# One row of W_down, loaded by transfers of 95 and 33 partitions, in a decode layer on one core

## The chip, the core and the metric

The kernel runs on one core of one Trainium2 chip. A core has a matrix engine (TensorE, PE in the profile; its weight loads are PEld), a vector engine (VectorE, DVE), a scalar engine (ScalarE, ACT), GpSimd (POOL) and a sync engine (SyncE, SP), which here only issues transfers. Sixteen DMA engines move data between HBM and SBUF. The metric is the device time of one execution, in microseconds.

## The reference

One decode step of a transformer layer, for 4 sequences with one new token each: attention over a cached window, then a gated MLP.

```python
# x: [4, 1, 576]; k_cache, v_cache: [4, 16, 16384, 128]; all bfloat16
q = layernorm(x) @ wq                  # 32 heads of 128
k, v = the last 4096 positions of the caches, each of the 16 heads used by 2 query heads
p = softmax(q k^T / sqrt(128))
h = x + (p v) @ wo
g = layernorm(h)
gate = g @ W_gate; up = g @ W_up       # [576, 4608] each
out = h + ((gate * (gate > 0)) * up) @ W_down      # W_down: [4608, 576]
```

The window of the two caches is 134 MB, wq and wo are 4.7 MB each, and W_gate, W_up and W_down 5.3 MB each. All of it is read once.

## The kernel before

All weights and the caches go through one large SBUF buffer, `pool`, of four slots. SP issues the loads one after the other, in the order of the list `transfers`, each when the part of the buffer that it overwrites is free: wq (two transfers), then 32 transfers of 4096 KB that alternate between a K and a V block of four heads, then wo, then W_gate and W_up (two transfers each), and at the end W_down in six pieces. Each entry of the list has a name, the key of a semaphore, what must have been done before it is issued, and a function that issues it. `prog_sync` walks through the list; the store of the result stands behind it in the same queue and waits for OUT0 and OUT1.

For each of the 16 K blocks, DVE transposes the block (L403), PE multiplies it with the queries (L466 and L468 are the helper that records every PE operation), DVE takes the row maximum, ACT the exponential, DVE transposes the probabilities, and PE multiplies them with the V block. After the last block PE multiplies with wo (the end of this is ATTN), DVE and ACT compute the second layer norm, PE multiplies with W_gate and W_up, ACT and DVE form the gated product `hh`, and DVE transposes it into `hhT`.

W_down is seen as 128 partitions of 36 rows of 576 values (1152 bytes): row j of partition p is row 36 p + j of the matrix. `WD` cuts the 36 rows into six pieces of 14, 9, 6, 4, 2 and 1 rows, each loaded by one transfer of all 128 partitions with a semaphore of its own (`wd0` to `wd5`). All six are issued by SP once ATTN is done, since they overwrite the region from which wo was read. PE's last loop goes through the pieces in that order: it waits for the landing of a piece and then makes two matmuls for each of its rows, which add up in PSUM. After the last row, ACT and DVE copy the two halves of the result to SBUF (OUT0, OUT1), and SP stores it.

A transfer's semaphore counts to 16 for each transfer. The method `dma` of the class `Sched` adds 16 to the count of the key at each issue, and a wait for a name waits for the count which that key has after the named transfer. So a wait for the last of three transfers with one key is a wait for 48.

Of the kernel before, what the change touches and what calls it, by code (L numbers as in the profile page):

```python
# [12 lines left out]
D = 576  # L13
# [24 lines left out]
JJ = 36  # L38
# [63 lines left out]
def bass_sequential_preLN__sliding_block_cached__glu_gated_reglu__decode_kernel(  # L102
# [12 lines left out]
    with ExitStack() as es:  # L115
        cnt = [0]

        def sb(name, shape, dt):
            return es.enter_context(nc.sbuf_tensor(name, shape, dt))

        pool = sb("pool", [128, NSLOT * QUAD], BF16)
# [79 lines left out]
        transfers = []  # L201
# [49 lines left out]

        wd_sb = pool[:, 0:FC * D].rearrange("p (j n) -> p j n", j=JJ)
        WD = [(0, 14), (14, 23), (23, 29), (29, 33), (33, 35), (35, 36)]
        for k, (f0, f1) in enumerate(WD):
            transfers.append((("wd", k), f"wd{k}", ["ATTN"],
                              lambda e, f0=f0, f1=f1: e.dma_start(
                                  out=pool[:, f0 * D:f1 * D], in_=B_W_down.rearrange("(p j) n -> p (j n)", j=JJ)[:, f0 * D:f1 * D])))

        def feat(c):
            return slice(c, c + 509, 4) if c < 4 else slice(512, D)  # L260
# [1 line left out]
        def land(name):  # L262
            return ("L",) + (name if isinstance(name, tuple) else (name,))
# [195 lines left out]
        def prog_pe(S):  # L459
# [133 lines left out]

            for k, (f0, f1) in enumerate(WD):
                deps = [land(("wd", k))]
# [44 lines left out]
```

## Time and profile before

| | |
|---|---|
| time, median of 3 runs | 377.71 us (377.62 to 377.88) |
| the profiled execution's own time | 378.56 us |
| its span | 377.2 us |
| PE, PEld busy | 302.2 us (80%), 73.0 us (19%) |
| DVE, ACT, POOL busy | 225.8 us (60%), 53.4 us (14%), 5.2 us (1%) |
| moved by DMA | 159.74 MB, mean 423 GB/s |
| DMA packets | 6506 |
| issue to landing, six pieces of W_down | 15.0, 17.7, 19.3, 20.2, 20.4, 20.3 us |

The span is the time from the first to the last instruction of the profiled execution; the execution's own time has what lies around it too. Busy time is the sum over an engine's instructions, and an engine can be busy without being what the others wait for. The landing of a transfer is the time when its semaphore has its full count. Each DMA packet is recorded with its queue, its start, its duration and its size, but without the number of the DMA engine that carried it.

### The profile page before, as it was taken

The page shows a single profiled execution, that of the slowest core. Times are in us where ns is not written, and L with a number is a line of the kernel's source. Part 1 is how long each engine was busy: PE and PEld are TensorE (multiplying, and loading weights), DVE is VectorE, ACT ScalarE, POOL GpSimd, SP SyncE. Part 2 cuts the span into 40 slices and gives each one's busy share as a digit, 9 for nine tenths or more (in the row PEclk, how much of TensorE's full clock was granted, in tenths as well). Part 3 has the DMA queues.
Part 4 walks back from the last instruction along what each step waited for, and adds up shares of the span by engine and source line. Part 5 has one row for each costly group of instructions (what it writes and reads, how often), then busy time and mean ns, then how long its engine had stood idle before and what let it go on. Part 6 is the DMA issues. An engine that isn't in the chain of part 4 may idle for free.

```text
span 377.2 us, 2603 instructions
## 1 busy us (share of the span) xinstructions
PE 302.2 (80%) x1432; PEld 73.0 (19%) x772; DVE 225.8 (60%) x165; ACT 53.4 (14%) x140; POOL 5.2 (1%) x15
## 2 busy tenths in 40 slices
PE   0509299969996999499969996899879996968667
PEld 0101022212221222022212221122112121212214
DVE  8046677595849493858476846666675768231230
ACT  2202402110220112002200220020202010101020
POOL 5000000000000000000000000000000000000000
PEclk9999789998999899989989997799959998996988
DMA  8999999999999999999999999999999999999996
GB/s 334 445 445 389 445 440 393 445 440 438 422 424 441 438 434 408 441 441 427 413 440 441 431 427 427 440 434 427 420 441 440 417 424 441 422 432 429 443 404 255
DMA packets 6506, 159.74 MB, mean 423 GB/s; under 512 B 728, under 2 KB 864, under 8 KB 1632
## 3 DMA queue, kind: packets, MB, share of 16 engines
q1 hardware_dynamic: 6488, 159.59, 98.8%
q8 instruction: 8, 0.13, 0.1%
q10 hardware_dynamic: 8, 0.00, 0.0%
q14 instruction: 2, 0.02, 0.0%
HBM read 159.58 MB, written 0.00 MB: 423 GB/s over the span
## 4 chain that ended last, share of the span: by engine, by line
DMA 47%; DVE 29%; PE 20%; ACT 3%; SPq 1%; issue 1%; DVEq 0%
DMA pool<-in_A_k_cache_dram 41%; DVE kT L403 20%; PE sc L466 7%; PE sc L468 6%; DMA pool<-in_B_W_down_dram 5%; DVE acc L420 4%; PE val L466 3%; PE val L468 3%; DVE own_sb L417 2%; DVE probT L414 2%; ACT P L338 2%; PE pb L466 1%; DVE o_bf L442 0%; ACT L338 0%; DVE rmx L406 0%
## 5 line engine op out<-in xcount | busy, mean ns | idle before, releaser
L403 DVE STREAM_TRANSPOSE kT<-pool 128x2048 f32<-128x2048 f32 x64 | 142.8, 2278 | 25.3 <-DMA pool<-in_A_k_cache_dram 24.3
L466 PE MATMUL sc<-kT,qz 128*128 128x512 bf16 x256 | 110.5, 432 | 36.6 <-DVE kT L403 36.3
L468 PE MATMUL sc<-kT,qz 128*128 128x512 bf16 x256 | 109.6, 428 | 0.0
L466 PE MATMUL val<-pool,probT 128*64 128x512 bf16 (+2 forms) x328 | 104.2, 374 | 4.4 <-DMA pool<-in_B_W_down_dram 4.4
L468 PE MATMUL val<-pool,probT 128*64 128x512 bf16 x256 | 96.2, 379 | 0.0
L466 PEld LDWEIGHTS sc<-kT,qz 128*128 128x128 bf16 x256 | 26.7, 104 | 146.5 <-issue 71.1
L466 PEld LDWEIGHTS val<-pool,probT 128*64 128x64 bf16 (+1 forms) x328 | 32.1, 107 | 81.3 <-issue 68.5
L406 DVE TENSOR_REDUCE rmx<-sc 128x1 f32<-128x1024 f32 x16 | 19.6, 1225 | 41.0 <-PE sc L468 41.0
L333 ACT ACTIVATE diag<-spot,rmx 128x16 f32<-128x16 f32 x16 | 4.9, 307 | 234.0 <-DVE rmx L406 234.0
L414 DVE STREAM_TRANSPOSE probT<-P 128x1024 bf16<-128x1024 bf16 x16 | 19.9, 1246 | 21.0 <-ACT P L338 21.0
L338 ACT ACTIVATE P<-sc,bias 128x1024 bf16<-128x1024 f32 x16 | 17.8, 1114 | 21.0 <-DVE bias L409 21.0
L327 ACT COPY qz<-qrep 32x128 bf16<-32x128 bf16 x64 | 18.8, 294 | 0.6
L409 DVE TENSOR_REDUCE bias<-pb 128x1 f32<-128x16 f32 x16 | 2.8, 175 | 23.8 <-PE pb L466 23.8
L420 DVE TENSOR_REDUCE acc<-own_sb 128x128 f32<-128x1024 f32 x8 | 15.2, 1897 | 0.3
L417 DVE TENSOR_TENSOR own_sb<-val,mask 128x1024 f32<-128x1024 f32 x8 | 9.6, 1200 | 7.9 <-PE val L468 7.9
L466 PE MATMUL sc<-pool,oX 128*4 128x288 bf16 x32 | 10.0, 338 | 0.4 <-ACT oX L347 0.4
L468 PE MATMUL sc<-pool,oX 128*4 128x288 bf16 x32 | 9.9, 336 | 0.0
L478 PE MATMUL pb<-ident_b,xn_bf 4*128 4x4 bf16 (+1 forms) x5 | 0.4, 180 | 10.0 <-DVE xn_bf L371 10.0
L466 PE MATMUL sc<-qT,sel 32*128 32x128 bf16 x4 | 0.3, 284 | 9.6 <-DVE qT L427 9.6
L445 DVE TENSOR_TENSOR h_row<-sc,x_bf 4x576 f32<-4x576 f32 x1 | 0.7, 745 | 11.6 <-PE sc L468 11.6
L466 PE MATMUL pb<-diag,same 128*128 128x16 f32 x32 | 6.3, 273 | 1.7 <-ACT diag L333 1.7
L466 PEld LDWEIGHTS pb<-diag,same 128*128 128x128 f32 x32 | 4.8, 188 | 11.8 <-ACT diag L333 7.4
(102 smaller groups left out, 85.7 us busy)
## 6 DMA issues: line engine op xcount, KB each, us to landing
pool<-in_A_k_cache_dram SPq DMA_DIRECT2D x16, 4096.0 KB, 26.8
pool<-in_A_v_cache_dram SPq DMA_DIRECT2D x16, 4096.0 KB, 26.4
pool<-in_A_wo_dram SPq DMA_DIRECT2D x1, 4608.0 KB, 18.3
pool<-in_B_W_gate_dram SPq DMA_DIRECT2D x1, 4608.0 KB, 18.6
pool<-in_B_W_up_dram SPq DMA_DIRECT2D x1, 4608.0 KB, 24.7
pool<-in_A_wq_dram SPq DMA_DIRECT2D x1, 4096.0 KB, 12.7
pool<-in_B_W_down_dram SPq DMA_DIRECT2D x1, 2016.0 KB, 15.0
pool<-in_B_W_down_dram SPq DMA_DIRECT2D x1, 1296.0 KB, 17.7
```

The costliest lines, as they stand in the source:

```text
L327: S.op(a, lambda e, src=src, dst=dst: e.copy(out=dst, in_=src), deps=deps, name=("QZ", i) if g == 3 else None, signal=g == 3)
L333: S.op(a, lambda e, i=i: e.activation(out=diag[:, i % 2, :], in_=spot[:, :], func=ACT.Copy, scale=rmx[:, i % 2:i % 2 + 1]), deps=[("RMAX", ...
L338: S.op(a, lambda e, i=i: e.activation(out=Pb[:, (i % 2) * 1024:(i % 2 + 1) * 1024], in_=sc[:, (i % 2) * 1024:(i % 2 + 1) * 1024], func=ACT ...
L403: S.op(v, lambda e: e.transpose(out=dst, in_=src), deps=deps, name=("TR", f))
L406: S.op(v, lambda e: e.tensor_reduce(out=rmx[:, i % 2:i % 2 + 1], in_=sc[:, (i % 2) * 1024:(i % 2 + 1) * 1024], axis=AX.X, op=ALU.max), dep ...
L409: S.op(v, lambda e: e.tensor_reduce(out=bias[:, i % 2:i % 2 + 1], in_=pb[TPB][:, 16 * (i % 2):16 * (i % 2) + 16], axis=AX.X, op=ALU.min), ...
L414: S.op(v, lambda e: e.transpose(out=pT[i % NPT], in_=Pb[:, (i % 2) * 1024:(i % 2 + 1) * 1024]), deps=[("EXP", i)] + ([("PV", i - NPT)] if ...
L417: S.op(v, lambda e: e.tensor_tensor(out=own_sb[:, :].rearrange("p (x d) -> p x d", d=DH), in0=val[:, :].rearrange("p (x d) -> p x d", d=DH ...
L420: S.op(v, lambda e: e.tensor_reduce(out=acc[:, w % 2, :], in_=own_sb[:, :].rearrange("p (x d) -> p d x", d=DH), axis=AX.X, op=ALU.add), de ...
L445: S.op(v, lambda e: e.tensor_tensor(out=h_row[:, :], in0=attn, in1=x_bf[:, :], op=ALU.add), deps=["ATTN", land("x")], name="H")
L466: return e.matmul(o, lhsT=l, rhs=r, start=start, stop=stop, skip_group_check=skip)
L468: return e.add_instruction(mybir.InstMatmult(name=nc.get_next_instruction_name(), start_tensor_calc=start, stop_tensor_calc=stop, bass_ski ...
```

## The change

The third piece of W_down, rows 23 to 28, is loaded as before but for its last row. Row 28 is loaded by two transfers of its own, issued ahead of the rest of the third piece: one for partitions 0 to 94, and one for partitions 95 to 127. All three count on the semaphore `wd2`, so PE's wait for the third piece is now one for a count of 48. The bytes, their places, all other transfers and all instructions of the other engines stay as they were. SP issues 47 loads where it issued 45.

```diff
         wd_sb = pool[:, 0:FC * D].rearrange("p (j n) -> p j n", j=JJ)
         WD = [(0, 14), (14, 23), (23, 29), (29, 33), (33, 35), (35, 36)]
+        wd_src = B_W_down.rearrange("(p j) n -> p (j n)", j=JJ)
+
+        def add_wd(name, key, f0, f1, p0, p1):
+            transfers.append((name, key, ["ATTN"], lambda e: e.dma_start(out=pool[p0:p1, f0 * D:f1 * D], in_=wd_src[p0:p1, f0 * D:f1 * D])))
+
         for k, (f0, f1) in enumerate(WD):
-            transfers.append((("wd", k), f"wd{k}", ["ATTN"],
-                              lambda e, f0=f0, f1=f1: e.dma_start(
-                                  out=pool[:, f0 * D:f1 * D], in_=B_W_down.rearrange("(p j) n -> p (j n)", j=JJ)[:, f0 * D:f1 * D])))
+            if k == 2:
+                add_wd(("wd", 6), "wd2", 28, 29, 0, 95)
+                add_wd(("wd", 7), "wd2", 28, 29, 95, 128)
+            add_wd(("wd", k), f"wd{k}", f0, f1 - (k == 2), 0, 128)
```

## The prediction

> **What bounds the kernel now.** I read the 40 slices first, then the chain of waits, then the timeline and the busy shares of the last ten microseconds, and last the queues and the landings. The slices of the page say that the DMA engines have no gap from the second slice to the last:
>
> ```profile
> DMA  8999999999999999999999999999999999999996
> GB/s 334 445 445 389 445 440 393 445 440 438 422 424 441 438 434 408 441 441 427 413 440 441 431 427 427 440 434 427 420 441 440 417 424 441 422 432 429 443 404 255
> ```
>
> PE and DVE are busy too, but nothing else is full from one end to the other, and only the last slice is half empty. So the time is the bytes at about 425 GB/s, plus what the tail adds. The chain of waits in time, from the issues of W_down on, confirms it:
>
> ```profile
> 353.78 20.18 DMA pool<-in_B_W_down_dram
> 374.00 0.70 PE val L466 x7
> 374.72 0.68 PE val L466 x5
> 375.42 0.42 DVE out_sb L456
> ```
>
> The fourth piece of W_down is in the queue from 353.78 to 373.96; then the fifth and sixth pieces land, PE does their products, DVE and ACT copy the result, and the store ends the span at 377.2. The timeline shows that PE waits for each piece:
>
> ```profile
> 367.48 4.95 PE L466 MATMUL val<-pool,probT 128*4 128x320 bf16 x46 [3.77 <-DMA pool<-in_B_W_down_dram]
> 372.63 0.98 PE L466 MATMUL val<-pool,probT 128*4 128x320 bf16 x12 [0.21 <-DMA pool<-in_B_W_down_dram]
> 374.00 1.38 PE L466 MATMUL val<-pool,probT 128*4 128x320 bf16 x14 [0.39 <-DMA pool<-in_B_W_down_dram]
> 375.42 0.42 DVE L456 CAST out_sb<-val 4x256 bf16<-4x256 f32 x1 [9.02 <-PE val L466]
> ```
>
> The last landing therefore sets the end, with a fixed 2.2 us behind it (375.03 to 377.2). Now the busy shares of that stretch (columns: window, its length, busy time of PE, PEld, DVE, ACT, POOL, then the granted clock, the DMA share and GB/s):
>
> ```profile
> 371.00:373.00 2.00, 1.79 (x26) 1.02 (x23) 0.00 (x0) 0.00 (x0) 0.00 (x0) 1.00 0.98 396
> 373.00:374.00 1.00, 0.61 (x11) 0.25 (x6) 0.00 (x0) 0.00 (x0) 0.00 (x0) 1.00 0.56 218
> 374.00:375.00 1.00, 0.98 (x12) 0.42 (x12) 0.00 (x0) 0.00 (x0) 0.00 (x0) 1.00 0.20 69
> ```
>
> The DMA share falls from 0.98 to 0.56 to 0.20 before the last byte is there: some of the 16 engines are done almost 2 us before the others. The landing counts say which share. A transfer's semaphore is raised once by each engine, and the trace keeps the 16 times. For the last piece, in us:
>
> ```
> 373.16 373.17 373.22 373.23 373.25 373.37 373.73 374.04 374.65 374.66 374.68 374.73 374.75 374.76 374.78 375.03
> ```
>
> Five engines are done within 0.09 us of each other, three follow by 374.04, seven come 1.5 us late at 374.65 to 374.78, and one at 375.03. The mean is 374.08: 0.95 us lies between it and the last, and that is all that any rearrangement of bytes could win. The queues say where the lateness is from:
>
> ```profile
> q1 hardware_dynamic: 6488, 159.59, 98.8%
> q8 instruction: 8, 0.13, 0.1%
> q10 hardware_dynamic: 8, 0.00, 0.0%
> ```
>
> The 8 packets of q8 are instruction fetches of 16 KB. By the packet records each occupies an engine for about 1.0 us (0.96 to 1.11) and lengthens the data packet behind it by about 0.5 us (0.47 to 0.55, in the six cases with a 32 KB packet behind); the group that lands 1.5 us late grows by about one engine with each. Eight fetches, eight late engines: each hit another one.
>
> **The change part by part.** *How the two transfers are cut.* q1 has 6488 packets: 45 loads of 128 partitions give 16 shares of 8 packets and 16 counts each (45 x 144 = 6480), and the store of 4 partitions gives 4 + 4. q10, the load of x with 4 partitions, gives 4 + 4 too. So shares are equal and there is one count per share. Equal shares of 95 partitions in at most 16 engines are 5 of 19; of 33, 11 of 3. I take that. The bounds are all 16 engines (6 rows on nearly all, and 2 to 3) and one engine.
>
> [...] No trace here shows an engine's number.
>
> *The price of a row.* The packet records have one row of 1152 B at a spacing of 47 ns from one packet's start to the next, 2304 B at 89, 4608 B at 174, 6912 B at 258. The third piece's packets go from six rows to five, 216 ns halfway between 174 and 258: 8 x 42 = 0.336 us less on every engine. One count costs 9 ns.
> - Engines with both extra shares: 22 x 47 + 18 - 336 = +0.716 us. If the 5 and the 11 are different engines instead: 19 x 47 + 9 - 336 = +0.566.
> - Engines with a share of 3 alone: 3 x 47 + 9 - 336 = -0.186 us.
> - Engines with none: -0.336 us.
>
> *Where these fall.* If the five with 19 rows are early ones, they end at 373.25 + 0.72 = 373.97, or 374.76 should the one at 374.04 be among them, and the late ones set the end: 375.03 - 0.19 = 374.85 if the last has a share of 3, 375.03 - 0.34 = 374.70 if it has none. The gain is 0.19 to 0.34 us; I take 0.26, the middle. If a late engine is among the five, it ends at 374.65 + 0.72 = 375.36 up to 375.03 + 0.72 = 375.75: a loss of 0.33 to 0.72 us.
>
> *SP.* Two more issues on SP, at 0.33 to 0.44 us each like the six around them: the eight end at about 356.0, not 355.2. The store, later in the same queue, waits for PE until 375.9 anyway. The cover is the backlog: the engines still move W_gate and W_up, whose last piece lands at 360.73 to 362.61. Cost zero; 0.9 us if the backlog were gone.
>
> *The wait.* PE now waits for three landings, a count of 48, ahead of row 23. Behind it in PE's queue stand the last 26 products and then the copies and the store. The two small transfers are ahead of the rest of the third piece in every ring, so the wait ends with that rest, 0.19 to 0.34 us earlier than 372.59 in the good case. There PE is the cover that runs out: its 46 products end at about 372.4, so only some 0.16 us can be used at that place; it does not matter, since 0.39 us of idle time stands before the next piece. The products are the same, and the fixed 2.2 us stays.
>
> *Sum.* The profiled execution took 378.56 (span 377.2), 0.85 over the median of 377.71. Minus 0.26 it is 378.30, and the median 377.45.
>
> **The rivals.**
> - *The extra rows fall on late engines* (slower): +0.33 to +0.72 us, 378.04 to 378.43; 378.2 with the seven at 374.78 (+0.46). It decides as soon as one late engine is among the five with 19 rows, for their slack is then under 0.72. For it: the trace numbers no engine, and if fetches go round in order and start anywhere, only 4 of 16 positions of a run of eight leave a given five untouched. Against it: exactly five engines form the early group, and instructions loaded ahead of the span (PE ran some 200 before the first fetch at 56.6 us) took places in that order before the eight seen.
> - *The split does not do what it says*: shares on all 16 engines, 6 + 3 rows at most against 8. 9 x 47 + 18 - 336 = +0.10 us: 377.8. Against it are the four counts of the 4-partition transfers. [...]
> - *One engine takes a whole transfer*: 95 x 47 = 4.5 us on one engine, less 0.34 saved and up to 1.8 of slack: +2.3 to +4.1 us, 380 or more. Nothing in the profile speaks for it but that no shape like 95 occurs.
>
> **How the numbers follow.** Extra rows on early engines 0.57, on late ones 0.32, on all 16 engines 0.07, on one 0.04. The likeliest gives 377.45. The range: from 377.71 - 0.34 less 0.1 for the scatter of the runs (377.62 to 377.88), 377.25, to the rival's worst, 378.43 and a little over, 378.5. It leaves out the single engine and little more. The likeliest case's own range is 377.25 to 377.6. A change under 0.2% (0.76 us) can hardly be told from none here. So the first case, the third and most of the second are no change; slower takes the single engine, those of the second whose late engine at 375.03 gets the rows and pays a little more, and what I have not seen: 0.15. Faster would need 0.76 of the 0.95 us there is, three times my gain: 0.05.
>
> **What would show it.** q1 has 6488 + 100 + 44 = 6632 packets with shares of 5 and 11 (6648 with 16 and 16). The new transfers leave 5 and 11 counts one by one. The last piece's landings: the early ones move to about 373.9, the last from 375.03 to 374.7 to 374.85, and the DMA share of 373 to 374 rises from 0.56. SP's eight issues stay at some 0.4 us each. The prediction is wrong if a landing comes after 375.03: then the rows sat on late engines; and if the fetches hit other engines from one execution to the next, the time will scatter by up to 1 us.

## The result, and the profile after

The changed kernel takes 378.61 us (median of 8 runs, 378.23 to 379.34), the kernel before 377.68 us beside it: a ratio of 1.0025, 95% interval 1.0014 to 1.0036. It is 0.93 us slower, where 0.26 us faster was forecast. That is above the range of 377.25 to 378.5, and a loss where a gain was forecast.

The profiled executions hide this at first: both have a span of 377.2 us. The one of before had its first piece of W_down landed only at 367.43 us. In the thirteen other traces of this study, the one after and a second one of the kernel before among them, it lands between 366.45 and 367.06. So I compare from that landing to the last one: 7.60 us before, 8.02 us after (366.95 to 374.97). In thirteen of the fourteen traces the execution's own time is the last landing plus 3.5 to 3.6 us.

The queues of the page after:

```profile
q1 hardware_dynamic: 6632, 159.59, 98.9%
q8 instruction: 8, 0.13, 0.1%
```

6632 packets is what the shares of 5 and 11 were to give. SP's first five issues of W_down in the chain of waits after, and then the wait for the fourth piece and the products:

```profile
351.80 0.33 SPq L257
352.17 0.43 SPq L257
352.65 0.38 SPq L257
353.07 0.29 SPq L257
353.41 0.36 SPq L257
353.81 20.09 DMA pool<-in_B_W_down_dram
373.94 0.70 PE val L472 x7
374.66 0.67 PE val L472 x5
```

Up to the fourth piece the transfers issue as fast as before, and the chain has the same form: a landing, then PE. The last two issues are not in the chain, and they are not as before. In the trace the issue of the fifth piece takes 2.38 us and that of the sixth 1.16, where 0.43 each was usual, and the eight end at 357.86. So the sixth piece stands in the queue for 18.3 us and no longer for 20.3 (KB, then us from issue to landing, of the fifth and the sixth piece after):

```profile
pool<-in_B_W_down_dram SPq DMA_DIRECT2D x1, 288.0 KB, 20.3
pool<-in_B_W_down_dram SPq DMA_DIRECT2D x1, 144.0 KB, 18.3
```

The first packet of the fifth piece moves at 371.77, long after its issue, so nothing waited for it. The loss is inside the 20 us in the queue. The busy shares of before and of after over the same stretch (window, length, PE, PEld, DVE, ACT, POOL, granted clock, DMA share, GB/s), before first:

```profile
366.00:368.00 2.00, 0.52 (x6) 0.40 (x8) 0.40 (x1) 0.00 (x0) 0.00 (x0) 0.87 1.00 422
368.00:370.00 2.00, 2.00 (x21) 1.49 (x17) 0.00 (x0) 0.00 (x0) 0.00 (x0) 0.50 0.96 406
370.00:371.00 1.00, 1.00 (x12) 0.53 (x8) 0.00 (x0) 0.00 (x0) 0.00 (x0) 0.55 0.98 410
```

```profile
366.00:368.00 2.00, 1.01 (x9) 0.79 (x11) 0.11 (x1) 0.00 (x0) 0.00 (x0) 0.56 0.95 400
368.00:370.00 2.00, 2.00 (x21) 1.38 (x17) 0.00 (x0) 0.00 (x0) 0.00 (x0) 0.59 1.02 289
370.00:371.00 1.00, 0.49 (x7) 0.12 (x6) 0.00 (x0) 0.00 (x0) 0.00 (x0) 1.00 1.02 365
373.00:374.00 1.00, 0.61 (x11) 0.25 (x7) 0.00 (x0) 0.00 (x0) 0.00 (x0) 1.00 0.78 301
```

Between 368 and 370 the DMA engines are as busy as ever (1.02) and move 289 GB/s instead of 406. The engines do not pause; the packets themselves are longer. Against before, 2 us x 117 + 1 us x 45 + 2 us x 22 GB/s = 323 KB are missing by 371, which is 0.76 us at 425 GB/s. The packet records say the same: a row of 1152 B, 51 ns long before, takes up to 95; a packet of 10368 B, which belongs to the untouched second piece, up to 648 instead of 389; one of 5760 B up to 399, where 220 is the usual. In the last line the share of 373 to 374 has risen from 0.56 to 0.78, as it was to do.

From those records each engine's packets can be strung together, since each starts where the one before ends (3 to 5 ns earlier for most), and the number of rows tells the three kinds of engine apart. The time of one engine from the start of its second piece to its last packet, with what the prediction's prices make of it (the typical engine of each kind; single ones are up to 0.07 higher):

```
                                    before   after   change   forecast   not forecast
five engines, 19 + 3 rows             7.69    9.12    +1.43      +0.72          +0.71
six engines, 3 rows                   7.69    8.23    +0.54      -0.19          +0.73
five engines, no row                  7.69    8.09    +0.40      -0.34          +0.74
```

So the differences between the three kinds are as forecast within 0.03 us, and every one of the 16 engines lost some 0.7 us besides (0.71 to 0.80).

### The profile page after: what moved, and what is told of

Its sections match the earlier page's. It is cut to its first block, busy times and chain, and to the rows that moved or that the text cites. A ratio compares the mean times of both kernels' runs of the same rounds, so it can differ in the third digit from the quotient of the medians.

```text
span 377.2 us, 2605 instructions
## 1 busy us (share of the span) xinstructions
PE 300.0 (80%) x1432; PEld 72.7 (19%) x772; DVE 225.7 (60%) x165; ACT 53.6 (14%) x140; POOL 5.2 (1%) x15
## 3 DMA queue, kind: packets, MB, share of 16 engines
q1 hardware_dynamic: 6632, 159.59, 98.9%
## 4 chain that ended last, share of the span: by engine, by line
DMA 46%; DVE 29%; PE 20%; ACT 3%; SPq 1%; issue 1%; DVEq 0%
DMA pool<-in_A_k_cache_dram 41%; DVE kT L409 20%; PE sc L472 7%; PE sc L474 6%; DMA pool<-in_B_W_down_dram 5%; DVE acc L426 4%; PE val L472 3%; PE val L474 3%; DVE own_sb L423 2%; DVE probT L420 2%; ACT P L344 2%; PE pb L472 1%; SPq L257 0%; DVE o_bf L448 0%; ACT L344 0%
## 5 line engine op out<-in xcount | busy, mean ns | idle before, releaser
L472 PE MATMUL sc<-kT,qz 128*128 128x512 bf16 x256 | 109.3, 427 | 38.1 <-DVE kT L409 37.8
L474 PE MATMUL sc<-kT,qz 128*128 128x512 bf16 x256 | 108.5, 424 | 0.0
L472 PE MATMUL sc<-pool,oX 128*4 128x288 bf16 x32 | 9.5, 325 | 0.4 <-ACT oX L353 0.4
L474 PE MATMUL sc<-pool,oX 128*4 128x288 bf16 x32 | 9.4, 326 | 0.0
## 6 DMA issues: line engine op xcount, KB each, us to landing
pool<-in_A_wo_dram SPq DMA_DIRECT2D x1, 4608.0 KB, 18.3
```

What stands on the lines that cost most here:

```text
L472: return e.matmul(o, lhsT=l, rhs=r, start=start, stop=stop, skip_group_check=skip)
L474: return e.add_instruction(mybir.InstMatmult(name=nc.get_next_instruction_name(), start_tensor_calc=start, stop_tensor_calc=stop, bass_ski ...
```

## The experiments

Three theories at the start. Theory 1, the prediction's main rival: the extra rows fall on engines that are late anyway. Theory 2: contention while the cut row is moved, on all engines. Theory 3: each further transfer costs. All kernels ran beside the kernel before (377.74 to 377.81 us). "Stretch" is the time from the last count of W_down's first piece to that of its last, 7.60 us in the first trace of before.

### Control, the changed kernel again, and two other cuts

The kernel before once more:

> The kernel before, once more, as a control: 377.7 us within 0.1. Its trace shows whether the spread of the last piece's landings (1.9 us, five early, eight late) comes back in another execution, and how far one profiled execution stands from the median.

377.86 us against 377.74 (ratio interval 0.9993 to 1.001). Stretch 7.57; every engine takes 7.68 to 7.70 us; the last landings are again five early, three between and eight late, 374.33 to 374.62. So the spread comes back in another execution. The miss of 0.06 is within the scatter: its runs, and those of before, go from 377.6 to 378.5.

The changed kernel again:

> The changed kernel again, for a second trace: 378.6 us, 0.9 over the kernel before. If the loss is the extra rows on late engines (theory 1), the five engines with 19 rows land last and the DMA rate stays at some 410 GB/s until they are alone. If the loss is contention while the cut row is moved (theory 2), the stretch after the second piece shows all engines busy at some 290 GB/s, as in the first trace, and rows of 1152 B that take 70 to 90 ns instead of 51.

378.64 us (1.0011 to 1.0029). The hole of 368 to 370, a full share with few bytes moved, is back at a DMA share of 0.98, while the last microsecond has a few engines alone:

```profile
368.00:370.00 2.00, 2.00 (x19) 1.16 (x15) 0.00 (x0) 0.00 (x0) 0.00 (x0) 0.67 0.98 295
373.00:374.00 1.00, 0.81 (x12) 0.44 (x8) 0.00 (x0) 0.00 (x0) 0.00 (x0) 1.00 0.76 290
374.00:375.00 1.00, 0.76 (x10) 0.39 (x12) 0.00 (x0) 0.00 (x0) 0.00 (x0) 1.00 0.14 50
```

By kind the engines take 9.19, 8.28 to 8.41 and 8.13 to 8.21 us: an excess of 0.77 to 0.9 on each (0.78 for the five). Here theory 1 has a part too. Four of the five engines with 19 rows are early or between, but the fifth begins the second piece at 365.66, close to the eight late ones (365.75 to 366.19). It ends last, at 374.84, half a microsecond after all others (374.34), and the stretch is 8.60 in place of 8.02.

The cut at 96, so that all engines have 8 rows:

```diff
-                add_wd(("wd", 6), "wd2", 28, 29, 0, 95)
-                add_wd(("wd", 7), "wd2", 28, 29, 95, 128)
+                add_wd(("wd", 6), "wd2", 28, 29, 0, 96)
+                add_wd(("wd", 7), "wd2", 28, 29, 96, 128)
```

> The same row cut at partition 96 instead of 95: 16 shares of 6 and 16 of 2, so every engine has 8 rows as before, but in other partitions than in a transfer of 128. Theory 1 (too many rows on engines that are late): no loss beyond the finer packets, 377.8 us. Theory 2 (contention from shares that lie in other partitions than usual): most of the loss stays, 378.2 to 378.6. Theory 3 (two transfers more on the queue): 378.6 as well, but then the next kernel loses half.

378.44 us (1.0003 to 1.002), stretch 8.10. Equal numbers of rows, and three quarters of the loss is there: theory 1 alone is out.

The row as one transfer of 128 partitions:

```diff
+                add_wd(("wd", 6), "wd2", 28, 29, 0, 128)
```

> Row 28 as one transfer of 128 partitions, ahead of the rest of the third piece: 16 shares of 8 in the usual places. By theories 1 and 2 only the finer packets are paid, 0.04 to 0.1 us: 377.8. By theory 3 (each further transfer costs) half of the loss: 378.15.

378.13 us (0.9996 to 1.0014), stretch 7.67, and every engine takes 7.73 to 7.75 us: the finer packets cost 0.04, as worked out. The median is 0.3 higher than the trace explains, as theory 3 would have it, but the interval holds no change; theory 3 is settled by the three further transfers of the steps of 4 below, and why this median is higher stays open. No packet of a row takes longer than 52 ns, so the size of the packets and the separate transfer are not the cause of the hole.

### Where does the contention come from?

The row cut in the middle:

```diff
+                add_wd(("wd", 6), "wd2", 28, 29, 0, 64)
+                add_wd(("wd", 7), "wd2", 28, 29, 64, 128)
```

> The row cut in the middle: 16 shares of 4 twice, 8 rows for every engine. If contention comes from shares in other partitions than the 128-partition transfer has, it is there too, somewhere between 0.1 and 0.7 us on every engine: 377.8 to 378.4. If only uneven numbers of rows cost, there is none: 377.8 and the ordinary 405 GB/s after the second piece.

378.56 us (1.001 to 1.0028), over the range I gave (377.8 to 378.4): a loss with 16 shares of 4 twice. Every engine takes 8.24 to 8.28 us, 0.56 more, of which 0.04 to 0.05 are the finer packets. Its windows from 368:

```profile
368.00:370.00 2.00, 1.42 (x10) 0.41 (x6) 0.00 (x0) 0.00 (x0) 0.00 (x0) 0.50 0.97 331
370.00:372.00 2.00, 1.69 (x16) 1.33 (x17) 0.00 (x0) 0.00 (x0) 0.00 (x0) 0.50 1.01 397
```

This is the one trace whose time is not the last landing plus 3.5 us, but plus 4.0. Its timeline:

```profile
370.31 5.34 PE L472 MATMUL val<-pool,probT 128*4 128x320 bf16 x44 [0.90 <-DMA pool<-in_B_W_down_dram]
375.70 0.41 ACT L364 CAST out_sb<-val 4x320 bf16<-4x320 f32 x1 [13.25 <-PE val L472]
```

PE waited 0.9 us for the second piece, which landed at 370.27. The clock granted to it was 0.50 until 374, and it ran 44 products without a further wait for data until 375.7, though the last piece had landed at 374.85. PE was the cover that ran out: some 0.45 us of this execution (378.82, the longest of its ten) are not the transfers'. How many of the other nine have that is not known.

The cut at 95 again, but with other rows as the source:

```diff
+        wd_near = B_W_down.rearrange("(p j) n -> p (j n)", j=2)
+        # the two transfers read wd_near[p0:p1, 0:D] instead of wd_src[p0:p1, 28 * D:29 * D]
```

> The cut of 95 and 33, but the two transfers read other rows of W_down, 2304 B apart instead of 41472 B (so the products of row 28 use other weights). If the contention is on the side of HBM, from where the rows lie, it changes: every engine's excess of 0.7 us between the second piece and the end falls or grows, and the time with it. If it is on the side of SBUF, nothing changes: 378.6, some 290 GB/s in the same stretch.

378.41 us (1.0007 to 1.0025). The engines take 9.22 to 9.25, 8.31 to 8.40 and 8.18 to 8.20 us, an excess of 0.8 to 0.9 on each. The rows lie 18 times closer in HBM and the contention is not smaller: the distance of the source rows is not what costs.

Now the destination. The kernel before with 15 more rows on five engines, in steps of 4 partitions, and the same in steps of 8:

```diff
+        FREE = FC * D
+        def add_extra(i):
+            transfers.append((("extra", i), "wd2", ["ATTN"], lambda e: e.dma_start(
+                out=pool[i:i + 17:4, FREE:FREE + 5 * D], in_=B_W_down.rearrange("(p j) n -> p (j n)", j=JJ)[i:i + 17:4, 0:5 * D])))
...
+            if k == 2:
+                for i in range(3):
+                    add_extra(i)
# in steps of 8: i:i + 33:8
```

> The kernel before with three more transfers of five partitions each (i, i+4, ..., i+16; 5760 B each, into a free part of the buffer), ahead of the third piece: 0.68 us more work for the five engines that carry a transfer of five shares, and no cut of the row. If these five engines are early, as the prediction had it, the time stays: 377.8, with the last landing where it was. If late ones are among them (the prediction's rival), 378.1 to 378.4. If the five shares lie in the engines' usual partitions, no packet takes longer than the 220 ns of a 5760 B packet.

> The same with partitions i, i+8, ..., i+32. The extra work per engine is equal, only the partitions differ. If contention depends on which partitions an engine writes, one of the two steps shows packets of 300 ns and an excess on all engines, and the other doesn't; without a dependence both look the same.

Steps of 4: 377.75 us against 377.78 (0.9986 to 1.0005), stretch 7.59. Steps of 8: 378.49 us (1.001 to 1.0029), stretch 8.05. First the window of the first, then of the second:

```profile
368.00:370.00 2.00, 0.97 (x14) 0.43 (x11) 0.00 (x0) 0.00 (x0) 0.00 (x0) 1.00 1.01 423
```

```profile
368.00:370.00 2.00, 0.85 (x12) 0.34 (x6) 0.00 (x0) 0.00 (x0) 0.00 (x0) 1.00 0.99 304
```

The same number of transfers, bytes and shares, and a rate of 423 or of 304 GB/s, by the partitions. (The source rows move with the partitions here, since row group i of W_down goes to partition i; with the cut row, other source rows had changed nothing.) In steps of 4 the five engines take 8.36 us each (+0.67, the sum gives 0.68), the other eleven 7.69 to 7.70 (nothing), and no 5760 B packet is longer than 225 ns. In steps of 8 a 5760 B packet takes up to 424 ns, the five engines 8.89 to 9.23 us, and the eleven 8.13 to 8.37: all pay. That the three further transfers in steps of 4 cost nothing also rules theory 3 out.

In steps of 4 from partition 64, the same with `64 + i`:

> The three further transfers of five partitions again, in steps of 4, but from partition 64 on (64+i to 80+i). The same five engines carry them and no two of the five share a group of partitions more than with a step of 4 from 0. If it costs to write any partitions that are not an engine's own, the packets grow past 300 ns and the time is 378.2 to 378.5, as with steps of 8; if only collisions among the five cost, it stays at 377.75.

378.91 us (1.0018 to 1.0036), the dearest of the three and over the range I gave (378.2 to 378.5): the five take 9.20 to 9.38 us, the eleven 8.54 to 8.85.

```profile
368.00:370.00 2.00, 2.00 (x20) 1.25 (x17) 0.00 (x0) 0.00 (x0) 0.00 (x0) 0.52 0.96 248
```

Steps of 4 from 0 and from 64 have the same distances at the source and at the destination. So steps of 4 are not what is free; partitions 0 to 18 in those steps are. Eight such transfers, with 32 to 35 as well (`for i in (0, 1, 2, 3, 32, 33, 34, 35)`):

> Eight of the transfers of five partitions in steps of 4 (from 0, 1, 2, 3, 32, 33, 34, 35): 1.8 us more work on the five engines, in place of 0.68 us. The late engines are behind the first of the five by some 1.5 us, and behind the last of them by 0.8 to 1.0 us; so the five now set the end: 378.1 to 378.8 if partitions 32 to 35 are as free of contention as 0 to 3, more if they are not.

378.71 us (1.0013 to 1.0031), as expected, and for the reason expected: the five take 9.47 to 9.48 us, 1.78 more (8 x 225 ns = 1.80), the eleven 7.69 to 7.70. The transfers that begin at 32 to 35 are as free as those that begin at 0 to 3. Here only the five engines' own end sets the time, and they had some 1 us to spare.

Which engine writes which partitions stands in no packet record. So the three patterns show that the partitions decide, 423 GB/s against 304 and 248, and not by what. That a share costs where it falls outside the partitions that its engine writes in a transfer of 128, as I had it in the expectations, is a guess that no trace shows.

### More of it, and at another place

Two rows cut at 95, `27, 29` for `28, 29`:

> Two rows, 27 and 28, cut at 95 in one pair of transfers (packets of 2304 B). Contention by the bytes that go to other engines' partitions: the excess on every engine about doubles, from 0.72 to 0.78 us to some 1.5 us; the engines with shares of 3 and without shares save 0.4 and 0.7 us, so the late ones end some 0.8 to 1.1 us after those of the kernel before, and the five early ones catch up with them: 378.9 to 379.4. If the contention is a fixed price of a cut, 0.7 on every engine less 0.4 to 0.7 of savings: 377.9 to 378.1.

379.85 us (1.0042 to 1.007), 2.0 over the kernel before, and stretch 9.85: over the range I gave. The cost grows with the bytes and is no fixed price of a cut. Its packets can be strung together with looser links: the five engines take 10.53 to 10.70 us, the six 8.85 to 9.20 and the other five 8.62 to 8.70. Against the prices that is an excess of 1.5 to 1.9 us on each, twice that of one row, as expected. The loss of time more than doubles because the last landings stand apart, 375.51, 375.81 and 376.30 us against 375.25 for the next, and the last two are of engines with 19 rows: their extra rows now exceed their lead, where I had them only catching up.

The cut on the last row, behind all else:

```diff
-            if k == 2:
+            if k == 5:
+                add_wd(("wd", 6), "wd5", 35, 36, 0, 95)
+                add_wd(("wd", 5), "wd5", 35, 36, 95, 128)
+            else:
+                add_wd(("wd", k), f"wd{k}", f0, f1, 0, 128)
```

> The cut of 95 and 33 on the last row, 35, behind all else. The early five are done 1.5 us before the late ones, so they carry their 19 rows while the late ones are still at the fourth and fifth piece. Without contention the last landing is 0.2 to 0.34 us earlier: 377.45. With contention that hits the late engines too it is up to 0.5 us later: 378.0 to 378.3. I expect the latter.

378.12 us (0.9999 to 1.0017), stretch 7.91: the least of the cuts at 95, and no gain. Two windows near its end, in which the cut row moves:

```profile
372.00:373.00 1.00, 0.77 (x12) 0.41 (x7) 0.00 (x0) 0.00 (x0) 0.00 (x0) 1.00 0.83 266
373.00:374.00 1.00, 0.42 (x8) 0.33 (x8) 0.00 (x0) 0.00 (x0) 0.00 (x0) 1.00 0.47 139
```

At a share of 0.83, 266 GB/s is 320 for full engines: the late engines still pay for what the early ones write. Strung together, the engines show it: the three without 19 rows that are done by 372.1 take 7.31, 7.45 and 7.45 us, within 0.01 of what the prices give, and the eight late ones 0.31 to 0.40 us more than that. None of the kernels beats the one before.

## Why the prediction was wrong, point by point

- **The bound** held: the last landing sets the end, and the end follows it by a fixed time in thirteen of fourteen traces.
- **The shares** were right: 6632 packets, and counts of 5 and of 11. The +0.72 us for an early engine put both shares on the same five, which no trace of before shows; in the first trace after, five engines carry 19 + 3 rows, six carry 3 and five none.
- **Where the rows fall** was right for the most part. In the nine traces that show the five engines (five cuts at 95, four of the steps), they are early or between the groups, and the eight late ones are always among the other eleven. The exception is one engine of one trace, which cost that execution 0.5 us. So the main rival, priced 0.33 to 0.72 us, is not the mechanism, though its range comes nearer to the result. Fifteen more rows on these engines, written where they cost nothing else, left the time at 377.75.
- **The price of a row is the step that failed.** "one row of 1152 B at a spacing of 47 ns" was read from a transfer of 128 partitions, in 16 shares of 8 rows that took 51 ns each. It was carried over to shares of 19 and of 3, and charged only to the engines that carry these rows. In the first trace a row of the cut takes 51 to 95 ns (61 to 72 for the middle one on the five engines), and packets of other transfers grow by up to two thirds (648 ns for 389) on engines that have no row at all. The term that is missing in the sum is some 0.72 us on every engine in the first trace, 0.8 to 0.9 in the other two cuts of this row. So the late engines, forecast at -0.34 to -0.19 us, measured +0.40 to +0.54 in the first trace; in the second, with one of the five late, the stretch grew by 1.0. The median of +0.9 lies between them.
- **Shares on all 16 engines**, the second rival, were priced at +0.10 us for 6 and 3 rows. The cuts at 96 and at 64, which have shares on all 16, measured +0.70 and +0.78 us, and the trace of the cut at 64 has 0.56 on every engine, of which the finer packets are 0.04 to 0.05. The price failed here too.
- **SP** cost nothing, but not as worked out. Six of the eight issues take 0.29 to 0.43 us, the last two 2.38 and 1.16, so that the eight end at 357.86 and not at about 356.0. In the three other traces with a cut at 95 in the third piece the issue of the fifth piece takes 2.5 to 3.0 us; in no other trace does an issue of W_down take more than 0.85. Why is open. The backlog covered it, which was the prediction's reason. **The wait** for a count of 48 cost nothing by itself either.
- **The sign** that was to show the prediction wrong, a landing after 375.03, did not come in the first trace: its last is at 374.97. 375.03 was of an execution whose first piece had landed 0.4 to 1.0 us later than in any other, so a time counted from the start of one execution could not show this loss. The stretch from landing to landing did.
- **The scatter**: its runs lie 1.1 us apart, from 378.23 to 379.34, those of before up to 0.9 in the larger samples. That agrees with the one late engine of the second trace, but no more than that is shown.

What stays open: the median loss of 0.93 us is 0.5 more than the stretch grew in the first trace and 0.1 less than in the second, and two traces of the changed kernel can't say how often one of the five is late, or how often PE at half clock adds to the time as it did with the cut in halves. Why engines that carry no row of the cut slow down by the same amount as the others (0.74 us against 0.71 and 0.73) was not tried.

## What to carry to other kernels

Before moving bytes between DMA engines to balance them, ask which cut the price of a packet was read from: 51 to 52 ns for a row in one transfer of 128 partitions was 51 to 95 in the cut at 95. That row of 147 KB, cut at 95 or 64 ahead of the rest of the third piece, slowed every engine by 0.5 to 0.9 us beyond the prices; as one transfer of 128 it cost 0.04. A window with a full DMA share and a low rate is the sign (1.02 with 289 GB/s, where before had 0.96 with 406): compare GB/s with the share, not the share alone.

## What the runs showed of the hardware

- Beside the same stream, three loads of five partitions with the same bytes and packets left 423 GB/s in a window (partitions 0 to 18 in steps of 4), 304 (steps of 8) or 248 (steps of 4 from partition 64). The slowdown reached all 16 engines, 0.71 to 0.80 us each in the changed kernel.
- Moving the source rows from 41472 B to 2304 B apart did not lessen it (an excess of 0.7 to 0.9 us on each engine before, 0.8 to 0.9 with it).
- In the first trace of before the 16 engines finish the last piece up to 1.9 us apart, eight of them 1.4 us or more behind the first five; eight fetches of instructions had taken 0.96 to 1.11 us each. Extra loads to partitions 0 to 18 in steps of 4, on five engines that are early or between, cost no time at 0.67 us each (377.75 against 377.78); with those to 32 to 51 as well it was 1.78 us each, and the time 378.71.
